# First quad of batch 2 transposed on TensorE, and w_out loaded in three parts with earlier sums, in a fused attention and MoE kernel

## The chip, the cores and the metric

The kernel runs on one core of one Trainium2 chip. The metric is the device time in microseconds (us). "Half clock" means that the trace's clock records grant TensorE 0.5 of full speed. "Ratio" always means: the mean time of one kernel's fast runs over the mean time of the fast runs of the kernel before in the same rounds, with a 95% interval. It is therefore not quite the ratio of the medians that are quoted beside it.

Engines: PE is TensorE's matmul row and PEld its weight loads, DVE is VectorE, ACT is ScalarE, POOL is GpSimd, SP is the engine that issues most DMAs.

## The reference

```python
# q, k, v: (8 batches, 12 heads, 448 rows, 64), float32
scores = q @ k.T / sqrt(64) - log(448)
attn_out = sigmoid(scores) @ v
x = attn_out.transpose(0, 2, 1, 3).reshape(3584, 768)
h = x @ w_in                 # w_in: 768 x 2048
g = h * sigmoid(h)
out = g @ w_out              # w_out: 2048 x 768
```

## The kernel before

Everything that TensorE reads is fp16. Four facts are needed to follow the argument.

1. **Attention runs beside the GEMMs.** Each batch has three "quads" of four heads. A quad's q and k are loaded by SP's DMA queue, cast to fp16 on GpSimd, and transposed, either on TensorE (early quads) or by a DMA transpose (batch 2 and later). One attention step makes scores (TensorE), a sigmoid (ScalarE) and, two steps later, products with v (TensorE). A step counter `n` (0 to 20 in a batch) also decides when loads and casts for the next batch are issued.
2. **Each batch has eight up-projections** (`h_pair`: 24 + 24 small matmuls, with an attention step between the halves). VectorE multiplies each result with its sigmoid.
3. **Output products come in groups of seven**, one group for each pair of neighbouring batches (0 and 1, 1 and 2, and so on), with sums in place of the eighth product. The sums of w_out (`sum_w`, eight half sums) are made once, beside batch 1's up-projections; the sums of g (`sum_g`, s_1 to s_4) are made in every group. All are VectorE instructions with both inputs in SBUF. The third product needs s_2 and one of the w_out sums.
4. **w_out and v are loaded through GpSimd's DMA queue**, which casts fp32 to fp16 on the way.

```python
def load_w_out():
    for n in range(2):                       # two halves of 1,024 rows, all 768 columns
        fc = slice(n * NFC // 2, (n + 1) * NFC // 2)
        f = slice(n * DFF // 2, (n + 1) * DFF // 2)
        nc.gpsimd.dma_start(w_out_sb[:, fc], moe_w_out[f].rearrange("(fc p) e -> p fc e", p=P))

def sum_w(step):                             # order: t3, t1, t2, t4, two halves of each
    ...
    x = (3, 1, 2, 4)[x]
    a, b = {3: (w22, w12), 1: (w12, w11), 2: (w22, w12), 4: (w21, t_sums[2])}[x]
    nc.vector.tensor_sub(t_sums[x][:, kk], a[:, kk], b[:, kk])

def o_group(b):
    ...
    sum_g(1)
    if b == 1:
        sum_w(4)
        sum_w(5)
    yield from mm(x, of_g(0, 0), w11)        # first product
    p1 = keep(x, "p1", "part1")              # VectorE copies PSUM to SBUF
    sum_g(2)
    yield from mm(y, of_g(0, 1), w21)        # second product
    halves(y, osb[0][:, :, lo], p1)
    sum_g(4)
    yield from mm(x, of_s(2), t_sums[2], start=False)   # third: needs s_2 and t2
    u2 = keep(x, "u2", "part1")
    sum_g(3)                                 # s_3 shares its tile with s_2
    yield from mm(y, of_s(1), t_sums[1])     # fourth
    ...                                      # fifth needs s_3; three more products

def gemm_stream():
    for b in range(B):
        for f2 in range(NFC // 2):
            for s in h_pair(b, f2):
                yield *s, b
            if b == 1 and f2 >= 4:
                sum_w(f2 - 4)
        ...

# end of batch 1's attention, then batch 2's first step
while s_done < N1:
    attend(next(places))                     # places: the PSUM tiles that scores go to
    attend_v(v_done + 4)
attend_v(N1)
early.close()
late = ctx.enter_context(tc.tile_pool(name="late", bufs=1))
attend()
```

## Time and profile before

| | before |
|---|---|
| time, three runs at the outset | 388.6 us median (387.33 to 390.58) |
| span of the profiled run (a run of 390.73 us) | 389.0 us |
| TensorE busy | 93% of the span |
| longest waits of TensorE | 12.6, 2.1 and 1.7 us |

The page of the kernel before, cut to its span, the busy time of the engines, and two rows of forty equal slices (9.7 us each): TensorE's busy tenths, and the clock granted to TensorE in tenths of full speed.

```profile
span 389.0 us, 16157 instructions
...
PE 362.8 (93%) x7496; PEld 265.9 (68%) x7496; DVE 197.8 (51%) x217; ACT 225.7 (58%) x234; POOL 58.4 (15%) x70
...
PE   7999982499799999999999999999999999999995
...
PEclk9999998599989999999999999999999999999998
```

TensorE is at 9 almost everywhere. The exceptions, but for the first and the last slice and an 8 in slice 6, are slices 7 and 8 (58 to 78 us), where it idles, with the clock row at 8 and 5 beside it, and slices 11 and 12, with an 8 in the clock row. The rest is TensorE work, so what is saved in these two places stays saved.

The waits of TensorE in the kernel before (total us, times, longest):

```profile
PE psc_0_0_1511 L197 <- DMA kT_0_1193<-xk_0_1191: 12.6, 1, 12.6
PE po_1_2060 L251 <- DVE s_1_2165 L352: 2.1, 1, 2.1
PE psc_2_3_1380 L197 <- ACT attnT_2_2_1372 L201: 1.7, 1, 1.7
```

The first line is the DMA transpose of batch 2's first key tile. The second is s_2, which the third output product needs. How they look in the timeline of TensorE (start, duration, line, output and inputs, and in brackets the idle time ahead and what ended it):

```profile
60.64 0.39 PE L216 MATMUL pav_2_1476<-attnT_2_6_1460,v_1_772 64*64 64x448 f16 x4
73.67 0.59 PE L197 MATMUL psc_0_0_1511<-qT_0_1189,kT_0_1193 64*64 64x448 f16 x4 [12.64 <-DMA kT_0_1193<-xk_0_1191]
74.04 2.41 PE L251 MATMUL ph_0_1522<-xT_1430,w_in_sb 64*64 64x448 f16 x24
76.58 1.33 PE L251 MATMUL ph_0_1522<-xT_1430,w_in_sb 64*64 64x448 f16 x24
77.73 1.30 PE L251 MATMUL ph_1_1582<-xT_1430,w_in_sb 64*64 64x448 f16 x24
...
106.08 1.93 PE L251 MATMUL po_1_2060<-t_1845,s_1_2165 64*64 64x384 f16 x32 [2.08 <-DVE s_1_2165 L352]
...
111.14 1.47 PE L251 MATMUL po_1_2061<-w_out_sb,s_1_2062 64*64 64x384 f16 x32
```

Behind each wait the same matmuls are slow: 24 matmuls take 2.41 us at 74.04 and 1.33 at 76.58. The trace's clock records give half clock from 66.0 to 76.3 us and from 107.0 to 110.4 us.

Why does that transpose take so long? DMA issues of the kernel before (output and input, queue, kind, count, us from issue to landing):

```profile
qT_0_1189<-xq_0_1187 SPq DMA_TRANSPOSE x1, 14.1
kT_0_1193<-xk_0_1191 SPq DMA_TRANSPOSE x1, 18.6
kT_1_1306<-xk_1_1304 SPq DMA_TRANSPOSE x1, 3.0
```

A like transfer takes 3 us a little later. The packet records of the trace, counted for stretches of four microseconds, show what differs: in the slow stretch w_out is being loaded, and the two queues move nearly the same number of packets.

```
from us   packets of SP's queue   packets of GpSimd's queue
56        439 (256 B)             454 (1,536 B)
64        456 (256 B)             452 (1,536 B)
```

(Up to 32 packets of 4 B are counted with each.) Finally VectorE ahead of the third product, in the kernel before:

```profile
99.53 1.68 DVE L350 TENSOR_TENSOR s_1_2062<-gT_736 128x1536 f16<-128x1536 f16 x1
101.14 0.41 DVE L350 TENSOR_TENSOR s_1_2062<-gT_1521 128x512 f16<-128x512 f16 x1
101.47 2.55 DVE L318 TENSOR_TENSOR t_1845<-w_out_sb 128x1536 f16<-128x1536 f16 x2
103.95 0.95 DVE L376 TENSOR_SCALAR p_1_2163<-po_1_2060 128x768 f32<-128x768 f32 x1
104.82 1.21 DVE L352 TENSOR_TENSOR s_1_2165<-s_1_2062,gT_736 128x2048 f16<-128x2048 f16 x1
```

```profile
98.77 1.64 POOL L160 CAST xq_1_2151<-stq_1_1746 128x896 f16<-128x896 f32 x1 [0.27 <-DMA stq_1_1746<-in_q_dram]
101.42 0.93 POOL L160 CAST xk_1_2155<-stk_1_1747 128x896 f16<-128x896 f32 x1 [1.01 <-DMA stk_1_1747<-in_k_dram]
```

The two w_out sums (t, 2.55 us together) stand in VectorE's queue between s_1 and s_2. A sum of 1,536 columns takes 0.95 us elsewhere in this trace, and 1.68 twice here, each time with a GpSimd cast at the same moment.

### The profile page before, as it was taken

How to read it: one execution, taken by the hardware profiler on the slowest of the kernel's cores; microseconds unless marked ns; L12 is line 12 of the kernel's file. 1: busy time of each engine (PE TensorE's matmuls, PEld its weight loads, DVE VectorE, ACT ScalarE, POOL GpSimd, SP SyncE). 2: the span in 40 equal slices, each digit the busy share in tenths (PEclk: the TensorE clock that was granted, in tenths of full speed). 3: DMA queues.
4: the chain of work that ended last, by engine and by line, in shares of the span. 5: the costliest groups of instructions: out<-in, count | busy, mean ns of one | idle time of the engine just before them, and what ended most of it. 6: DMA issues, size and time to landing. Idle time of an engine off the chain costs nothing.

```text
span 389.0 us, 16157 instructions
## 1 busy us (share of the span) xinstructions
PE 362.8 (93%) x7496; PEld 265.9 (68%) x7496; DVE 197.8 (51%) x217; ACT 225.7 (58%) x234; POOL 58.4 (15%) x70
## 2 busy tenths in 40 slices
PE   7999982499799999999999999999999999999995
PEld 4665541266566778877788778877788778876763
DVE  3445433046964357544673338533573446644672
ACT  2987892277444776657654776657755676634200
POOL 4232410120320111002120022001110000000000
PEclk9999998599989999999999999999999999999998
DMA  8999999879963966379551976369580600032005
GB/s 268 245 223 229 199 235 182 171 164 209 232 88 68 267 142 152 44 149 288 140 92 42 278 157 145 51 117 294 110 147 3 165 2 3 4 96 70 2 2 162
DMA packets 63731, 54.81 MB, mean 141 GB/s; under 512 B 35504, under 2 KB 60336, under 8 KB 63664
## 3 DMA queue, kind: packets, MB, share of 16 engines
q1 hardware_dynamic: 50528, 40.05, 43.1%
q0 software_dynamic: 12368, 12.49, 21.0%
q8 instruction: 58, 0.95, 1.0%
q10 hardware_dynamic: 768, 1.25, 0.9%
q14 instruction: 9, 0.07, 0.1%
HBM read 46.99 MB, written 11.01 MB: 149 GB/s over the span
## 4 chain that ended last, share of the span: by engine, by line
PE 80%; DMA 8%; DVE 5%; ACT 4%; issue 0%; POOL 0%; SPq 0%; POOLq 0%; DVEq 0%
DMA kT_0_1193<-xk_0_1191 5%; PE po_6_7981 L251 3%; PE po_5_6814 L251 3%; PE po_4_5628 L251 3%; PE po_2_3252 L251 3%; PE po_3_4440 L251 3%; DMA stk_0_1047<-in_k_dram 3%; PE po_1_2060 L251 2%; PE po_3_4441 L251 2%; PE po_2_3253 L251 2%; PE po_6_7982 L251 2%; PE po_4_5629 L251 2%; PE po_5_6815 L251 2%; PE po_1_2061 L251 1%; PE po_7_8838 L275 1%; DMA stq_0_90<-in_q_dram 1%
## 5 line engine op out<-in xcount | busy, mean ns | idle before, releaser
L251 PEld LDWEIGHTS <-w_in_sb 64*64 64x64 f16 x2688 | 88.3, 107 | 41.3 <-ACTq L266 10.0
L275 PEld LDWEIGHTS <-w_in_sb 128*64 128x64 f16 x192 | 12.5, 110 | 5.9 <-issue 0.3
L197 PE MATMUL psc_0_0_1511<-qT_0_1189,kT_0_1193 64*64 64x448 f16 x4 | 0.6, 578 | 12.6 <-DMA kT_0_1193<-xk_0_1191 12.6
L197 PEld LDWEIGHTS <-kT_0_1193 64*64 64x64 f16 x28 | 0.9, 119 | 13.6 <-DMA kT_0_1193<-xk_0_1191 13.1
L251 PEld LDWEIGHTS <-gT_6282 64*64 64x64 f16 x160 | 9.6, 107 | 0.9 <-ACTq L266 0.2
L102 PEld LDWEIGHTS <-zeros 64*64 64x64 f16 x192 | 6.5, 119 | 5.3 <-issue 2.4
L297 DVE TENSOR_TENSOR gT_1521<-ph_0_1522,tsig_0_1579 128x896 f16<-128x896 f32 x1 | 1.1, 1091 | 16.7 <-ACT tsig_0_1579 L296 16.7
L201 ACT ACTIVATE attnT_0_0_1510<-psc_0_0_1511,bias_s 128x896 f16<-128x896 f32 x1 | 1.0, 1007 | 14.0 <-PE psc_0_0_1511 L197 14.0
L251 PEld LDWEIGHTS <-gT_2720 64*64 64x64 f16 x176 | 8.1, 107 | 1.4 <-ACTq L266 0.5
L251 PEld LDWEIGHTS <-gT_1521 64*64 64x64 f16 x176 | 8.1, 107 | 1.1 <-ACTq L266 0.3
L251 PEld LDWEIGHTS <-gT_736 64*64 64x64 f16 x176 | 6.2, 107 | 2.6 <-issue 0.8
L251 PEld LDWEIGHTS <-gT_5096 64*64 64x64 f16 x160 | 6.6, 107 | 1.4 <-ACTq L266 0.5
L251 PEld LDWEIGHTS <-gT_3908 64*64 64x64 f16 x176 | 6.5, 107 | 1.2 <-ACTq L266 0.5
L251 PEld LDWEIGHTS <-gT_7467 64*64 64x64 f16 x128 | 6.1, 107 | 1.0 <-ACTq L266 0.5
L275 PEld LDWEIGHTS <-gT_8611 128*64 128x64 f16 x80 | 5.9, 110 | 1.2
L251 PE MATMUL po_1_2060<-t_1845,s_1_2165 64*64 64x384 f16 x64 | 4.3, 428 | 2.1 <-DVE s_1_2165 L352 2.1
L112 POOL DMA_DIRECT2D w_in_sb<-in_moe_w_in_dram x8 | 5.3, 673 | 0.0
L251 PEld LDWEIGHTS <-s_1_2165 64*64 64x64 f16 x64 | 2.4, 140 | 4.0 <-DVE s_1_2165 L352 2.5
L102 PE MATMUL pz_start<-zeros 64*64 64x448 f16 x44 | 4.0, 540 | 1.2 <-DVE bias_s L80 1.2
L201 ACT ACTIVATE attnT_0_0_204<-psc_0_0_205,bias_s 128x896 f16<-128x896 f32 x1 | 1.0, 1007 | 5.5 <-PE psc_0_0_205 L197 5.5
L160 POOL CAST xq_1_1300<-stq_1_1195 128x896 f16<-128x896 f32 x1 | 0.9, 933 | 20.4 <-DMA stq_1_1195<-in_q_dram 20.4
L251 PE MATMUL po_1_2061<-w_out_sb,gT_736 64*64 64x384 f16 x64 | 3.4, 324 | 0.4 <-issue 0.4
(1057 smaller groups left out, 1077.9 us busy)
## 6 DMA issues: line engine op xcount, KB each, us to landing
w_in_sb<-in_moe_w_in_dram POOLq DMA_DIRECT2D x8, 384.0 KB, 11.2
w_out_sb<-in_moe_w_out_dram POOLq DMA_DIRECT2D x2, 1536.0 KB, 27.4
out_dram<-osb_0_2058 SPq DMA_DIRECT2D x4, 192.0 KB, 3.2
out_dram<-osb_1_2059 SPq DMA_DIRECT2D x4, 192.0 KB, 7.5
out_dram<-osb_0_3250 SPq DMA_DIRECT2D x4, 192.0 KB, 3.9
out_dram<-osb_1_3251 SPq DMA_DIRECT2D x4, 192.0 KB, 8.0
out_dram<-osb_0_4438 SPq DMA_DIRECT2D x4, 192.0 KB, 3.5
out_dram<-osb_1_4439 SPq DMA_DIRECT2D x4, 192.0 KB, 7.9
```

Source lines behind the costliest of these rows:

```text
L102: nc.tensor.matmul(pz[half(t), j, :S], zeros[half(j), :D], zeros[half(j)], start=True, stop=True)
L112: nc.gpsimd.dma_start(w_in_sb[half(t), :, f], moe_w_in[t * NCC * D : (t + 1) * NCC * D, f].rearrange("(c d) f -> d c f", d=D),)
L160: eng.tensor_copy(x16[:, :, tt, :], st[:, tt].rearrange("p t (r d) -> p r t d", r=R))
L197: nc.tensor.matmul(psc[half(j), t, :S], kT[half(t), r, half(j)], qT[half(t), :, half(j)], start=True, stop=True,)
L201: return nc.scalar.activation(attn[b, i, r], psc[:, :, :S], AF.Sigmoid, bias=bias_s, scale=QKSCALE)
L251: mm = nc.tensor.matmul(out_of(u)[half(c)], lhs(u, k, c)[half(row)], rhs(u, k)[half(row)], start=(start and ph == 0 and k == 0), stop=(ph ...
L275: nc.tensor.matmul(out_of(u)[half(c)], lhs(u, k, c), rhs(u, k), start=(start and k == 0), stop=(k == nk - 1), skip_group_check=partial,)
L297: nc.vector.tensor_mul(gTs[b][:, 2 * f2 : 2 * f2 + 2, :], ph[:, :, :S], tsig)
```

## The change

The intent: take the DMA transpose off the path by transposing batch 2's first quad on TensorE, move its first two scores into the first up-projection of batch 1, stage the other quads sooner, swap the PSUM places of batch 1's last scores, and let w_out arrive in an order in which its sums can begin one product sooner.

```diff
     def load_w_out():
-        for n in range(2):
-            fc = slice(n * NFC // 2, (n + 1) * NFC // 2)
-            f = slice(n * DFF // 2, (n + 1) * DFF // 2)
+        for f, e0, e1 in ((0, 0, DMODEL), (1, NO2, DMODEL), (1, 0, NO2)):
+            rows = moe_w_out[f * DFF // 2 : (f + 1) * DFF // 2, e0:e1]
             nc.gpsimd.dma_start(
-                w_out_sb[:, fc], moe_w_out[f].rearrange("(fc p) e -> p fc e", p=P)
+                w_out_sb[:, f * NFC // 2 : (f + 1) * NFC // 2, e0:e1],
+                rows.rearrange("(fc p) e -> p fc e", p=P),
             )
...
         if b == 1:
-            sum_w(4)
             sum_w(5)
...
-                if b == 1 and f2 >= 4:
-                    sum_w(f2 - 4)
+                if b == 1 and f2 >= 3:
+                    sum_w(f2 - 3)
...
-            n_stage, n_cast = ((8, 11, 14), (11, 14, 17)) if b == 1 else ((0, 4, 8), (6, 10, 14))
+            n_stage, n_cast = ((8, 10, 13), (11, 13, 16)) if b == 1 else ((0, 4, 8), (6, 10, 14))
...
                         cast(b + 1, i2, nm, nc.gpsimd)
-                        transpose_dma(b + 1, i2, nm)
+                        if (b + 1, i2) != (2, 0):
+                            transpose_dma(b + 1, i2, nm)
...
-    places = itertools.cycle((ps_sc, ps_2[0]))
+    places = itertools.cycle((ps_2[0], ps_sc))
...
-    attend()
+    transpose_pe(2, 0, "qk")
...
-            if share == 0.5:
+            if share == 0.5 or (share == 1 and s_done == N1 + 1):
                 attend()
```

## The prediction

> **What bounds the kernel.** TensorE: the page gives it 93% of a 389.0 us span, and 80% of the chain of waits. Two places are not TensorE work.
>
> 1. After batch 1's last value product (61.0 us) TensorE idles 12.64 us, to 73.67, for the DMA transpose of batch 2's first key tile (waits view; 18.6 us from issue to landing, where later ones take 3). Its input was cast by 55.0. In the DMA records of 56 to 70 us the queue of the transposes and that of the casting loads (v, then w_out) each move about 113 packets per us: they alternate, so 1,792 packets of 256 B need about 16 us behind w_out's 1,536 B packets. The Trainium skill ("DMA: Bandwidth & Descriptors", Queues, rings and completion order) says that an engine round-robins at packet granularity; the trace agrees. The clock records show half clock from 66.1 to 76.3 us; the next half up-projection takes 2.24 us instead of 1.14.
> 2. At 104 us TensorE waits 2.08 us for VectorE (s_1_2165, behind two w_out sums of 2.55 us together), and half clock follows from 107.1 to 110.5: that output product takes 5.06 us, its like 3.36, 1.7 us lost. "TensorE: Matmul & The Clock Gate" (Part 1) describes this fall after an idle window.
>
> **What the change does.** Batch 2's first quad is transposed on TensorE: 28 transposes, 0.98 us in the trace for quad (1,2), and two VectorE copies of 0.62. Its first score moves into the first up-projection, the second to its end. The sums start one product earlier, so one (0.95 to 1.7 us) leaves the chain before s_1_2165. Batch 1's last four scores swap PSUM places, which removes part of a 1.73 us wait for ScalarE at 54.4; ScalarE then bounds, so about 0.5 us. Quads 1 and 2 are staged sooner. w_out's second half becomes two loads of 768 B packets (estimate 79 ns each, from 87 at 896 B and 134 at 1,536 B): about 1.5 us more DMA time.
>
> **On the critical path.** Transposes run at about 60.4 to 61.4 us; batch 1's second up-projection starts at about 64.4 instead of 77.7: 13.3 us. VectorE's sum: 1.2. No half clock at 107: 1.7. Sum 16.2 us. The rest is TensorE work and keeps the gain.
>
> **New deadlines**, estimated from the packet rates: w_out's upper right quarter lands at about 72, is wanted by VectorE at 72, and hurts TensorE only after 76; the last quarter lands at 80, needed at 86; quad 1's transposes at 72, needed at 78; quad 2's at 84, needed at 95.
>
> **Predicted time:** 372.5 us, 8 in 10 between 370 and 377. Chances: faster by over 2% 0.94, within 2% 0.05, slower 0.01.
>
> **Right if** TensorE waits under 1 us between 60 and 64 us; the second up-projection of batch 1 starts at 64 to 65; no half-clock record lies between 60 and 110; the wait before the third output product falls to about 0.9 us; later distances between products are unchanged. **Wrong if** VectorE waits for w_out near 72 and that reaches TensorE at the seventh up-projection; or TensorE waits for quad 1's transposes near 78, or batch 3's near 108; or half clock returns.
>
> **What would make it wrong.** In the freed time w_out was loading: if small packets, or staging that now shares the engines with v and w_out, delay w_out over 4 us more than I estimate, 2 to 5 us come back through VectorE's sums. A remaining VectorE wait that still brings half clock would return 1.7 us.

## The result and the profile after

The changed kernel took 374.53 us median (373.28 to 375.08, four runs) beside 388.95 us (387.33 to 390.58, four runs); ratio 0.9625, interval 0.9576 to 0.9674. The profiled run took 375.08 us, with a span of 373.2 us.

The page after, the same rows as before:

```profile
span 373.2 us, 16215 instructions
...
PE 361.8 (97%) x7524; PEld 274.4 (74%) x7524; DVE 199.0 (53%) x219; ACT 225.3 (60%) x234; POOL 59.2 (16%) x71
...
PE   7999999999899999999999999999999999999995
...
PEclk9999999999999999999999999999999999999999
```

TensorE's busy time is nearly the same (361.8 for 362.8 us, with 28 transposes more and less half clock in it), so 14.8 of the 15.8 us that the span lost are idle time. Both dips of the clock row are gone. One slice has an 8 left in it. The waits of TensorE after, from 40 us to 110 us, where the change lies:

```profile
PE psc L198 <- ACT attnT L202: 1.1, 2, 0.8
PE pav L217 <- DVE xT L229: 1.0, 1, 1.0
...
PE po L252 <- DVE s L353: 0.5, 1, 0.5
```

The 12.6 us wait does not appear, and the wait for s_2 (line 353) is 0.5 us instead of 2.1. The second line is **new**: a value product waits 1.0 us for VectorE's copy of x. TensorE's timeline after:

```profile
59.47 0.58 PE L180 MATMUL ptr_qk<-ident,xq 128*64 128x128 f16 x14
59.89 0.56 PE L180 MATMUL ptr_qk<-ident,xk 128*64 128x128 f16 x14
60.38 1.33 PE L252 MATMUL ph<-xT,w_in_sb 64*64 64x448 f16 x24
...
63.54 1.33 PE L252 MATMUL ph<-xT,w_in_sb 64*64 64x448 f16 x24
...
90.13 1.49 PE L252 MATMUL po<-t,s 64*64 64x384 f16 x32 [0.52 <-DVE s L353]
...
98.41 0.38 PE L217 MATMUL pav<-attnT,v 64*64 64x448 f16 x4 [1.00 <-DVE xT L229]
```

The transposes cost 0.9 us (59.47 to 60.38), and the up-projection behind them runs at full clock. The start of each landmark in the two timelines, and what the change had gained by then:

| landmark | before | after | gained so far |
|---|---|---|---|
| second up-projection of batch 1 starts | 77.73 | 63.54 | 14.2 us |
| third output product starts | 106.08 | 90.13 | 16.0 us |
| fourth output product starts | 111.14 | 93.93 | 17.2 us |
| fifth output product starts | 114.50 | 98.60 | 15.9 us |
| end of the span | 389.0 | 373.2 | 15.8 us |

So 1.3 us is given back between the fourth and the fifth product. VectorE there, and GpSimd beside it, after:

```profile
94.78 1.50 DVE L355 TENSOR_TENSOR s<-gT 128x1536 f16<-128x1536 f16 x1
96.21 1.15 DVE L355 TENSOR_TENSOR s<-gT,gT 128x512 f16<-128x512 f16 x1
97.28 1.08 DVE L229 TENSOR_SCALAR xT<-pav 128x896 f16<-128x896 f32 x1
```

```profile
94.55 0.93 POOL L161 CAST xk<-stk 128x896 f16<-128x896 f32 x1 [0.29 <-DMA stk<-in_k_dram]
95.73 1.35 POOL L161 CAST xq<-stq 128x896 f16<-128x896 f32 x1 [0.25 <-DMA stq<-in_q_dram]
97.03 1.12 POOL L161 CAST xk<-stk 128x896 f16<-128x896 f32 x1
```

s_3 takes 1.50 and 1.15 us instead of 0.95 and 0.41, beside GpSimd casts of batch 3, and the copy of x stands behind it in VectorE's queue. This is the same slowing that s_1 and the w_out sum had in the trace of before. There it lay in VectorE's chain ahead of s_2 and lengthened TensorE's wait for it; here it lies ahead of the copy of x.

The swap of PSUM places was not run on its own. In the traces TensorE's wait for ScalarE at batch 1's last scores fell from 1.73 to 0.78 us, and the last value product of batch 1 came 0.95 us sooner, counted from the second half of batch 0's last up-projection.

The new deadlines. The key transpose of quad 1 after:

```profile
kT<-xk SPq DMA_TRANSPOSE x1, 12.6
```

Issued at 62.47 us, it landed at about 75.1 us and was used at 78.47. w_out's parts landed at about 63.2, 69.8 and 76.2 us (issue plus time to landing), and no VectorE wait for w_out appears. The closest deadline was one that the forecast thought wide: quad 2's key transpose, issued at 79.92, took 12.2 us and landed at 92.1 us, for a score at 93.55 us.

### The profile page after: what moved, and what is told of

It is laid out like the page before. It is cut to its first block, busy times and chain, and to the rows that moved or that the text cites. A ratio compares the mean times of both kernels' runs of the same rounds, so it can differ in the third digit from the quotient of the medians.

```text
span 373.2 us, 16215 instructions
## 1 busy us (share of the span) xinstructions
PE 361.8 (97%) x7524; PEld 274.4 (74%) x7524; DVE 199.0 (53%) x219; ACT 225.3 (60%) x234; POOL 59.2 (16%) x71
## 4 chain that ended last, share of the span: by engine, by line
PE 86%; DVE 6%; ACT 5%; DMA 1%; issue 1%; SPq 0%; DVEq 0%
PE ph L252 33%; PE po L252 27%; PE psc L198 8%; PE pav L217 8%; PE ph L276 5%; ACT attnT L202 4%; PE po L276 4%; DMA stq<-in_q_dram 1%; ACT tsig L297 1%; DVE gT L298 1%; DVE xT L229 1%; PE ptr_qk L180 1%; DVE s L355 1%; DVE s L351 1%; DVE s L353 1%
## 5 line engine op out<-in xcount | busy, mean ns | idle before, releaser
L202 ACT ACTIVATE attnT<-psc,bias_s 128x896 f16<-128x896 f32 x168 | 166.1, 1008 | 96.4 <-PE psc L198 95.4
L252 PE MATMUL ph<-xT,w_in_sb 64*64 64x448 f16 x2688 | 142.0, 349 | 0.5 <-issue 0.3
L298 DVE TENSOR_TENSOR gT<-ph,tsig 128x896 f16<-128x896 f32 x64 | 69.8, 1091 | 99.2 <-ACT tsig L297 99.2
L297 ACT ACTIVATE tsig<-ph 128x896 f16<-128x896 f32 x64 | 58.7, 917 | 28.1 <-PE ph L276 14.1
L198 PE MATMUL psc<-qT,kT 64*64 64x448 f16 x672 | 65.3, 351 | 2.8 <-ACT attnT L202 2.1
L252 PEld LDWEIGHTS <-s 64*64 64x64 f16 x1536 | 54.5, 107 | 11.6 <-ACTq L267 3.7
L217 PE MATMUL pav<-attnT,v 64*64 64x448 f16 x672 | 58.3, 349 | 1.1 <-DVE xT L229 1.0
L252 PEld LDWEIGHTS <-gT 64*64 64x64 f16 x1152 | 41.2, 107 | 7.4 <-ACTq L267 2.8
L252 PE MATMUL po<-t,s 64*64 64x384 f16 x768 | 36.4, 323 | 0.7 <-DVE s L353 0.5
L252 PE MATMUL po<-w_out_sb,s 64*64 64x384 f16 x768 | 36.3, 323 | 0.0
L229 DVE TENSOR_SCALAR xT<-pav 128x896 f16<-128x896 f32 x24 | 26.1, 1087 | 16.2 <-PE pav L217 16.2
L276 PEld LDWEIGHTS <-w_in_sb 128*64 128x64 f16 x192 | 12.5, 110 | 5.9 <-issue 0.3
L379 DVE SCALAR_TENSOR_TENSOR osb<-po,u 128x768 f32<-128x768 f32 (+1 forms) x8 | 6.9, 858 | 15.9 <-PE po L252 14.4
## 6 DMA issues: line engine op xcount, KB each, us to landing
v<-in_v_dram POOLq DMA_DIRECT2D x8, 672.0 KB, 11.9
```

The costliest lines, as they stand in the source:

```text
L198: nc.tensor.matmul(psc[half(j), t, :S], kT[half(t), r, half(j)], qT[half(t), :, half(j)], start=True, stop=True,)
L202: return nc.scalar.activation(attn[b, i, r], psc[:, :, :S], AF.Sigmoid, bias=bias_s, scale=QKSCALE)
L217: nc.tensor.matmul(pav[half(t), j, :S], v16s[b][half(j), t, i, r * D : (r + 1) * D], attnT[half(j), t, :], start=(r == 0), stop=(r == R - 1),)
L229: nc.vector.tensor_scalar_mul(xTs[b][:, 2 * i : 2 * i + 2, :], pav[:, :, :S], SX)
L252: mm = nc.tensor.matmul(out_of(u)[half(c)], lhs(u, k, c)[half(row)], rhs(u, k)[half(row)], start=(start and ph == 0 and k == 0), stop=(ph ...
L276: nc.tensor.matmul(out_of(u)[half(c)], lhs(u, k, c), rhs(u, k), start=(start and k == 0), stop=(k == nk - 1), skip_group_check=partial,)
```

## The experiments

My theory after the result: (1) moving the transposes is nearly all of the gain; (2) the sums are worth about 1 us, the half clock behind them more, but not in every run; (3) the transposes were slow because two DMA queues alternate packet by packet; (4) the new 1.0 us wait comes from VectorE and GpSimd getting in each other's way. The main rivals: w_out's new order is what makes it work; the DMA transpose is slow by itself; the slow matmuls behind the wait wait for data, not for the clock.

Twelve kernels ran, in three calls of four. All gave correct results. Runs of one call share the runs of the kernel before: 387.43, 387.11 and 388.73 us median (11 runs each; two of the second call, 390.81 and 390.93 us, count as slow and are not in the ratios; without them its median is 386.58).

### Transposes alone

The kernel before, with only this:

```diff
-                        transpose_dma(b + 1, i2, nm)
+                        if (b + 1, i2) != (2, 0):
+                            transpose_dma(b + 1, i2, nm)
...
-    attend()
+    transpose_pe(2, 0, "qk")
...
-            if share == 0.5:
+            if share == 0.5 or (share == 1 and s_done == N1 + 1):
```

> The kernel before with one part of the change: quad 0 of batch 2 transposed on TensorE, its scores a step later. My theory: this part is nearly all of the gain. The 12.6 us wait goes, 1.0 us of transposes comes in, and the half clock at 66 to 76 us goes: 13 us off, about 375.5 us, ratio about 0.967. VectorE's sums are as before, so a wait of about 2 us in front of the third output product of batches 0 and 1 stays, and may bring half clock again. Rival: w_out's order is what makes the transposes pay. Then w_out's second half, in one piece, lands after the fifth up-projection wants its first sum (about 76 us), and TensorE waits 2 us or more for VectorE near 79 us, with a time over 378 us.

Measured: 375.55 us median (374.8 to 379.0), ratio 0.9717 (0.9675 to 0.9759). By the medians 11.9 us of the gain are here. The big wait and the half clock of 66 to 76 us are gone; the wait for s_2 is 1.47 us (in this trace a cast only touched s_2, which took 1.29 us) and no half clock follows. VectorE never waited for w_out, though it came in two pieces. The rival falls. Two of the six runs took 379 us, and the median hides them; see the run with two loads.

### w_out and sums alone

The kernel before with only the w_out and `sum_w` parts of the diff.

> The kernel before with only the other part: w_out in three loads, sums begun one product sooner; the DMA transposes stay. My theory: the 12.6 us wait stays (11 to 14 us); only the wait of 2.08 us in front of the third output product shrinks to 1 us or less and the half clock after it goes: 2 to 3 us off, about 386.3 us, ratio about 0.993. Rival: smaller w_out packets let the alternating transposes through sooner, so that the big wait itself shrinks: over 1 us shorter, and a time under 385 us.

Measured: 383.26 us (382.88 to 385.31), ratio 0.9905 (0.987 to 0.9939): 4.2 us by the medians, more than my 2 to 3. The rival was right here. The longest wait of TensorE in this run:

```profile
PE psc L198 <- DMA kT<-xk: 7.9, 1, 7.9
```

That is 4.7 us less than in the trace of before, with the same DMA transposes: the key tile took 12.5 us from issue to landing. From 64 to 68 us the packet records count 733 packets of SP's queue (60 of them already 1,792 B packets of the next load) beside 723 of w_out's queue, now of 768 B; with 1,536 B it was 456 beside 452. If two queues take turns, halving the other's packets speeds up one's own. In the traces the change's two parts eat into the same wait, which is gone in the first and 4.7 us shorter here, so this part cannot count twice. The whole times do not show that clearly: by the ratios the parts give 2.8% and 1.0%, and the whole change, which also has the swap of PSUM places, 3.8% in the first measurement and 3.4% in the next.

### w_out out of the transposes' way

```diff
             if n == 9:
                 load_v(2)
-                load_w_out()
...
                         cast(b + 1, i2, nm, nc.gpsimd)
                         transpose_dma(b + 1, i2, nm)
+                    if (b + 1, i2) == (2, 1):
+                        load_w_out()
```

> The kernel before with one move: w_out is loaded behind the casts of batch 2's quad 1, so not beside the transposes of quad 0; these stay DMA transposes. Theory of the two queues that alternate packet by packet: the two transposes now take 3 to 6 us from issue to landing instead of 14 and 18.6, and TensorE's wait at 61 us falls from 12.6 to under 2 us. w_out then lands 10 us or more too late for the first sum (wanted near 76 us), so 3 to 6 us come back as a wait for VectorE's sums: 380 to 384 us, ratio about 0.98. Rival: a DMA transpose is slow by itself in this place, and the wait stays over 8 us with w_out gone.

Measured: 390.41 us, the median of five fast runs (387.78 to 391.33), ratio 1.006 (1.0021 to 1.0098). The sixth, of 394.21 us, was slow and is not in the ratio. The two transposes of quad 0 now took:

```profile
qT<-xq SPq DMA_TRANSPOSE x1, 3.0
kT<-xk SPq DMA_TRANSPOSE x1, 2.9
```

With no load on the other queue a DMA transpose takes 3 us, so it is not slow by itself; and the 12.6 us wait is gone. My figure for the price was wrong: I had said 3 to 6 us. VectorE's first sum and TensorE behind it waited:

```profile
DVE t L318 <- DMA w_out_sb<-in_moe_w_out_dram: 11.2, 1, 11.2
```

```profile
PE ph L251 <- DVE gT L297: 10.0, 1, 10.0
```

w_out was now issued at 61.8 us, met the loads and transposes of quad 2 on the other queue, and its second half landed 24.5 us after issue. TensorE also waited 3.8 us for s_2, and half clock fell from 83.1 to 93.4 and from 103.6 to 110.5 us. The wait moved from one reader of the DMA engines to another. This is what the forecast feared of the change itself, and why doing the transpose on TensorE is worth so much: it takes 1,792 packets out of the alternation instead of moving them.

### The clock, first try

```diff
+    idle(12, "warm")         # 48 matmuls of zeros
     early.close()
```

> The kernel before with 48 matmuls of zeros put into the 12.6 us wait (about 9 us of TensorE work that nobody needs). The wait for the transposes stays where it was. My theory of the clock: no half-clock record near 66 to 76 us, the next half up-projection takes 1.14 to 1.3 us instead of 2.24, and 1.1 us is saved: about 387.8 us, ratio about 0.997. Rival: the slow up-projection has another cause than the clock (data arriving late), and it stays at 2.2 us.

Measured: 388.88 us (386.97 to 391.88), ratio 1.0038 (0.9997 to 1.0079). The run did not test what it should: the 48 matmuls took 2.46 us, since four run side by side, and the clock records give half clock from 66.2 to 76.5 us as before. Nothing follows for the clock. It did show two other things. With the DMA order of before, from the end of the last value product to the first score of batch 2 it was 11.9 us here, 12.6 us in the trace of before and 11.4 us in the next run, so the big wait varies by more than a microsecond. And the wait for s_2 was 2.75 us with no half clock behind it, where 2.08 us had one in the trace of before (why, see the clock below).

### The clock, mended

```diff
+    idle(50, "warm")         # 200 matmuls of zeros
     early.close()
```

> The run that kept TensorE busy in the big wait, mended: 48 matmuls of zeros took only 2.5 us there, since four of them run side by side, and the clock fell all the same. Now 200 of them, 9.5 us, end at about 71 us. Clock theory: no half clock between 60 and 80 us, the half up-projection behind the wait takes 1.3 us instead of 2.4, 1.1 to 1.7 us off the kernel before, ratio about 0.996. The wait for the DMA transposes ends where it did. Rival: the up-projection stays at 2.4 us.

Measured: 389.35 us (387.92 to 390.57), ratio 1.0011 (0.9974 to 1.0048). In the trace the matmuls of zeros ran from 61.19 us for 9.65 us, no half clock was granted until 104.1 us, and the half up-projection behind the wait:

```profile
71.62 1.30 PE L251 MATMUL ph<-xT,w_in_sb 64*64 64x448 f16 x24
```

That is 1.30 us instead of 2.41, so the slow matmuls were the clock. The time did not get shorter, though the mean clock of all six runs rose (0.993 to 1.0; in the kernel before 0.980 to 0.987 in the same call), and I cannot show why. The key tile landed 0.57 us after the last of the zeros in this trace; in runs where it lands sooner, the zeros themselves would be in the way. That is argued, not shown. For the change it means: by the traces the clock's part of the first gain is 1.1 us; no whole time shows it, and the interval here leaves room for about 1 us.

### The changed kernel once more

> The changed kernel once more, as the measure for the other runs of this call. Expected: 373 to 375 us, ratio 0.962 to 0.967; the wait of TensorE in front of the third output product of batches 0 and 1 about 0.5 us, and the new wait of a value product for VectorE about 1.0 us, if the casts of batch 3 on GpSimd fall where they fell in the first trace.

Measured: 374.3 us (373.62 to 375.14), ratio 0.9663 (0.9614 to 0.9712). The wait for s_2 is 0.52 us again; the wait for the copy of x is 0.45 us this time: in this trace s_3's first part took 0.95 us and its second 1.15, so one cast fell on it and not two. The half clock came in no place but the last microseconds.

### The sums moved back

The changed kernel with the two `sum_w` edits undone.

> The changed kernel with the sums of w_out begun where they were (after the fifth product, two of them left in front of the third output product). My theory: one sum of 0.95 us comes back into VectorE's chain, TensorE's wait there grows from 0.5 to about 1.5 us, and no half clock follows[...]: about 1 us slower than the changed kernel. Rival, the forecast's own sum: the half clock returns as well and the cost is 2.9 us.

Measured: 375.3 us (375.14 to 378.38), ratio 0.9698 (0.9649 to 0.9747): 1.0 us above the changed kernel of the same call by the medians. TensorE's wait for s_2 is 1.39 us and no half clock follows in the trace. The term is one sum, as in my theory; the forecast's 2.9 us (sum and half clock) is too much for this kernel.

### s_3 early

s_3 gets its own tile and is made while VectorE idles ahead of the copy of the third product.

```diff
-    tag=f"s{2 if x == 3 else x}"
+    tag=f"s{x}"
...
         sum_g(4)
+        sum_g(3)
         yield from mm(x, of_s(2), t_sums[2], start=False)
         u2 = keep(x, "u2", "part1")
-        sum_g(3)
```

> The changed kernel with the third sum of g (s3) in a tile of its own and computed ahead of the copy of the third product, while VectorE has nothing to do. Theory: the new wait of 1.0 us (a value product for the copy of batch 2's x) exists because s3 was slowed by GpSimd's casts from 1.36 to 2.65 us and stood in front of that copy in VectorE's queue; it goes, 1.0 to 1.3 us off the changed kernel. Rival: the copy was late for another reason (the values themselves); then the wait stays at about 1 us and the time is the same.

Measured: 373.85 us (373.38 to 374.76), ratio 0.9652 (0.9609 to 0.9695): 0.45 us below the changed kernel of the same call by the medians, whose wait for the copy was 0.45 us. In the trace that wait is gone, s_3 takes 0.96 and 0.42 us, and VectorE, free in time, idles 1.10 us until the values are there and then copies, so it was s_3 that had made the copy late. In time the difference is too small for these runs to prove.

### s_3 early, and all sums of t2 out of the way

```diff
         sum_g(1)
-        if b == 1:
-            sum_w(5)
...
-                if b == 1 and f2 >= 3:
-                    sum_w(f2 - 3)
+                if b == 1 and f2 >= 2:
+                    sum_w(f2 - 2)
```

(on top of the previous edit)

> As the run with s3 early, and the sums of w_out begun two products sooner than in the kernel before, so that none is left in front of s_1. Theory: w_out's upper right quarter lands at about 70 us and the first sum is now asked for at about 71 us at the earliest, so VectorE waits little; the remaining wait of 0.5 us in front of the third output product goes too: 1.5 to 1.9 us off the changed kernel, about 372.5 us, ratio about 0.961. Rival: the quarter lands later, VectorE waits for it, and the gain over the run with s3 early is nil or negative.

Measured: 372.72 us (372.13 to 375.06), ratio 0.9628 (0.9581 to 0.9675). Both VectorE waits are gone from TensorE's list between 40 and 110 us, and VectorE did not wait for w_out at 71.26 us. This is the fastest kernel: 1.6 us below the changed kernel of the same call by the medians. Five of its six runs are faster than every run of that kernel, one (375.06) is not, and the two ratios' intervals overlap, so the step is likely but small.

### GpSimd reading, and GpSimd only writing

Both put one useless GpSimd instruction beside the w_out sum and s_2 of the changed kernel, released as s_1 ends. (Batch 3's casts are emitted later in both, so that it can stand ahead of them in GpSimd's queue.)

```diff
+    scr = late.tile([P, 1792], F16, ...)     # scratch
...
         sum_g(1)
         if b == 1:
+            nc.vector.tensor_copy(scr1, scr[:, :1])                        # releases GpSimd
+            nc.gpsimd.tensor_copy(scr, v16s[2]...[:, :1792])                # the run that reads
+            nc.gpsimd.memset(scr, 1.0)                                      # or: the run that writes
             sum_w(5)
```

> The changed kernel with one useless GpSimd copy (1,792 fp16 columns out of SBUF into a scratch tile, about 1.9 us) released by VectorE as s_1 ends, in front of the last w_out sum and s_2, both sums with two inputs in SBUF. Theory of the shared SBUF port: GpSimd gets its turn after the w_out sum and holds the port through the start of s_2, so s_2 takes 1.2 us longer or starts as late, and TensorE's wait in front of the third output product grows from 0.5 to about 1.4 us: 0.9 us slower than its twin that only writes, about 375.2 us. Rival: the slow sums of the traces had another cause; then s_2 stays at 1.22 us and the wait at 0.5.

> The twin of the reading run: the same place, the same release, the same scratch tile, but GpSimd fills it with a constant instead of copying, so it reads nothing from SBUF. Theory (the Trainium skill, SBUF - State Buffer: a two-input VectorE instruction contends with a GpSimd instruction that reads SBUF, not with one that only writes it): the w_out sum stays at 0.95 us, s_2 at 1.22 us and the wait at about 0.6 us (0.1 for the small copy that releases GpSimd). Time as the changed kernel, about 374.3 us. Rival: any GpSimd work on SBUF slows these sums; then it is as slow as its twin.

Measured, in the traces, s_2 of the reading run and the copy beside it:

```profile
88.66 1.83 DVE L353 TENSOR_TENSOR s<-s,gT 128x2048 f16<-128x2048 f16 x1
87.08 2.33 POOL L408 COPY scr<-v 128x1792 f16<-128x1792 f16 x1 [5.12 <-DVE scr L407]
```

and s_2 of the writing run, with the fill and the cast (of batch 3) that followed it:

```profile
89.01 1.21 DVE L353 TENSOR_TENSOR s<-s,gT 128x2048 f16<-128x2048 f16 x1
87.42 1.59 POOL L408 MEMSET scr<- 128x1792 f16 x1 [4.83 <-DVE scr L407]
88.95 2.06 POOL L161 CAST xq<-stq 128x896 f16<-128x896 f32 x1
```

TensorE's wait for s_2 is 1.19 us in the first and 0.58 us in the second. In the reading run s_2 began while the copy ran and took 1.83 us instead of 1.22: a GpSimd read in progress slows a VectorE sum with two SBUF inputs that begins meanwhile. The size was 0.6 us instead of my 0.9.

The twin does not test what it should. Its fill ended at 89.01 us, just as s_2 began, and what ran beside s_2 was a cast, which reads. The sum was not slowed, and the cast took 2.06 us instead of 0.93. A read that begins within a running sum is itself the one delayed (the copy of the reading run began at 87.08 us, within the w_out sum of 86.93 us, which kept its 0.95 us); where the two begin within 0.06 us of each other, either may be: here it was the cast, at 101.4 us in the trace of before the sum. That a fill would not slow a sum is not shown: in no trace here does such a sum begin during a fill. All that the traces show of fills is that they did not wait for a running sum: three of them (at 79.59 us in the reading run, at 80.23 and 87.42 us in the writing run) began within one, and each took 1.59 us.

In whole times the twins do not differ: 373.91 us (ratio 0.9628, 0.9591 to 0.9665) and 373.99 us (0.9614, 0.9578 to 0.965). Six and five runs do not resolve 0.6 us; only the traces carry this conclusion.

### w_out in two loads

The changed kernel with the first part of the diff undone.

> The changed kernel with w_out in two loads as before, of 1,536 B packets. My theory now, after the run with w_out and sums alone in which the 768 B packets let 185 transpose packets per us through instead of 113: the split matters in two ways, but here neither is on the critical path. The second half lands in one piece at about 76 us, the first sum (asked for at 74.2 us) waits up to 2 us, and TensorE needs the product of that up-projection only at about 77 us: the same time within 0.5 us, ratio 0.964 to 0.968. Rival: the transposes of quad 1 (needed at 77 to 79 us) or the first sum come late enough for TensorE to wait 1 us or more.

Measured: 374.01 us (372.69 to 378.14), ratio 0.9629 (0.9583 to 0.9675): the same. With the transposes on TensorE, the order and packet size of w_out make no difference to the time that these runs could show. VectorE did not wait for w_out in this trace either.

The profile fell on the run of 378.14 us, and shows what such a run is made of. Batch 3's casts began at 87.03 us, in the middle of the sums, and fell on all of them:

```profile
87.22 2.75 DVE L350 TENSOR_TENSOR s<-gT 128x1536 f16<-128x1536 f16 x2
89.90 1.68 DVE L318 TENSOR_TENSOR t<-w_out_sb 128x1536 f16<-128x1536 f16 x1
```

s_1 took 2.75 us (1.29 in the traces of the changed kernel) and the w_out sum 1.68 (0.95). TensorE waited 2.72 us for s_2, and half clock followed from 93.8 to 97.2 us. The runs of 378 to 379 us among the transposes alone and the sums moved back look alike in time, but they were not profiled and their cause is open. One of them (378.86 us, mean clock 1.0) had no half clock at all, so not all of them can be like this one.

## Why the prediction was right

The measured 374.53 us lies in the stated range of 370 to 377, on the forecast's side of 2%. Point by point:

- **The big wait.** Forecast: 13.3 us by the start of the second up-projection, which would fall at 64.4 us. The traces give 14.2 us and 63.54 us. About half a microsecond of that lies ahead of 54 us, where the two traces already differ by it, and 0.95 us came with the swap of PSUM places (forecast 0.5). The transposes alone are 11.9 us by the medians.
- **The sums.** Forecast: 1.2 us of the wait for s_2, leaving 0.9. The wait fell from 2.08 to 0.52, but the trace of before had two casts on these sums and the trace of after had none: s_1 and two w_out sums took 4.5 us in the trace of before and 3.0 us in that of the transposes alone. Undoing the edit costs 1.0 us, one sum.
- **The half clock at 107 us, the mis-sized term.** Forecast: 1.7 us. In the kernel before it is a matter of chance: whether it comes hangs on where in time the wait falls (see the clock below). Over the 31 fast runs of that kernel the mean granted clock falls into two groups: 16 runs at 0.976 to 0.982 with a median of 388.81 us, and 15 at 0.986 to 0.991 with 387.07 us. The profiled run, 0.980 and 390.73 us, is of the first. That this half clock is what parts the groups is not shown, since none of these runs was profiled and half clock elsewhere counts in the mean too. I read all terms from this one trace and took them off the median of all runs. Taken off the run that they were read from, the same 16.2 us give 374.5 us, beside 375.08 us of the profiled run after. Between the medians the gain was 14.4 us. That the sum of 16.2 us lies so near the 15.8 us between the two traced spans is in part luck: up to the fourth product the change had gained 17.2 us, 1.0 more than forecast, and the next point took 1.3 back.
- **What came back.** The forecast had no term for the collision of batch 3's casts with s_3: 1.3 us of delay to the fifth product in the first trace after, 0.45 us of waiting in the second. Its rule "later distances between products are unchanged" failed here.
- **The w_out loads.** The forecast counted smaller packets as a cost of 1.5 us of DMA time. The packets took 78 ns, as estimated (79), but the run with w_out and sums alone shows them to be a help to whoever shares the engines with them. In the whole change neither shows.
- **The deadlines.** w_out's parts landed at 69.8 and 76.2 us (forecast 72 and 80), quad 1's key tile at 75.1 (72), quad 2's at 92.1 (84, with its score at 93.55). The last had 1.4 us to spare, not eleven.

On the clock, the Trainium skill ("TensorE: Matmul & The Clock Gate", Part 1) says that the clock falls after at least one idle window of about 3.4 us and that the window is free-running. The half-clock records here, but for those at a program's very end, are 3.41 us or whole multiples of it, which agrees. A whole idle window was not needed, though. Waits of 2.08, 2.47 and 2.72 us were enough in three traces, and 2.75 us was not in a fourth. The traces settle why, if the time of each is cut into steps of 3.41 us that end where its half-clock records begin and end. The three waits each lie within one step, and half clock begins as that step ends; so it does at 62.3 us in the run with w_out and sums alone, after a step with 2.02 us of idle time. The wait of 2.75 us straddles a border at 103.8 us, with 0.71 us before it and 2.04 us behind it. So about 2 us of idle time within one step brought half clock here, and the length of a wait alone does not tell (2.02 us did and 2.04 us did not, so the border lies about there; a step of 1.37 us of idle time at the start of one program, before 8.4 us, does not fit). Waits of 1.4 us or less, as in the runs of the changed kernel but for the one of 378.14 us, are too short for it.

The forecast cited the same page for the fall after the 2.08 us wait; the page asks for a longer idle time.

On VectorE and GpSimd, "SBUF — State Buffer", Who interferes with whom, says that a VectorE instruction with two SBUF inputs contends with a GpSimd instruction that reads SBUF, not with one that only writes. The reading run agrees with the first half (s_2 of 1.83 us instead of 1.22); no run here shows the second.

## What to carry to other kernels

Where two DMA queues were busy here, a transfer of many small packets went at the pace of the other queue's packets (a transpose of 3 us took 18.6). Doing that piece on an engine that waits for it anyway, or making the other's packets smaller, paid; reordering the two only moved the wait. Before terms of one trace are added up, ask whether the traced run is typical (its time and its mean clock against the other runs), and take the sum off that run. When a change shifts the schedule, look for two-input VectorE work with a GpSimd read beside it in both traces: such a collision may leave one place and reappear in another.

## What the Trainium skill lacked or had wrong

- "DMA: Bandwidth & Descriptors" (Queues, rings and completion order) says that an engine drains a packet of about 9 to 17 descriptors typically before it switches queues. It gives no figure for what this does to a transfer of short records. Here the two queues moved nearly equal numbers of the trace's packets (456 beside 452, 733 beside 723 in 4 us), and a DMA transpose of 3 us took 18.6 us beside 1,536 B packets and 12.5 us where they were of 768 B from about 60 us on.
- "DMA: Bandwidth & Descriptors" has a bandwidth for DMA transposes, but no page that I read has the time from issue to landing of a small SBUF-to-SBUF one: 3 us for 128 x 896 fp16 with no load beside it.
- "TensorE: Matmul & The Clock Gate" asks for an idle window of about 3.4 us and advises against gaps over about 3 us. Here 2.02 to 2.72 us of idle time within one window of 3.41 us was enough, and a wait of 2.75 us that two windows shared was not. Past the first 20 us, waits up to 1.73 us were never followed by half clock.
- "SBUF — State Buffer" was right that such VectorE sums and GpSimd reads contend. A size for it in a real kernel is missing: beside a cast, sums of 0.95 us took up to 1.70 us, short ones of 0.41 us up to 1.15 us, and casts of 0.93 us up to 2.06 us.
